# Efficient attention, FNet mix and MLP on one core: second layers of orders 2 to 7 add their results to x by accumulating transfers

## The chip, the core and the metric

The kernel runs on one core of one Trainium2 chip. The metric is the time of one execution on the device in microseconds (us). The kernel before was run 3 times: median 1003.57 us, from 1002.22 to 1005.59. One execution more was taken with the hardware profiler; all views of the trace below are of that one.

## The reference

The inputs are q, k, v of 8 batches, 8 heads, 576 tokens and 64 columns per head, and the weights of an MLP, 512 x 2048 and 2048 x 512; all of it is fp32.

```python
q_s = softmax(q, over the 64 columns); k_s = softmax(k, over the 576 tokens)
kv  = k_s^T v                    # 64 x 64 for each head
x   = q_s kv                     # put side by side: (8, 576, 512)
u   = x + real(fft2(x))          # over tokens and columns
un  = (u - mean(u)) / sqrt(var(u) + 1e-6)
out = u + relu(un @ w_ch1) @ w_ch2
```

The two products of the last line are by far the largest part of the work: 4608 tokens by 512 by 2048, twice.

## The kernel before

**Groups and orders.** The 4608 tokens are taken in nine groups of 512. Group g = 0 to 7 holds 512 of the 576 tokens of batch g; group 8 holds the 64 that each batch leaves over (its tokens lie in tiles called xs, those of a batch in tiles called x). The groups are worked off in the sequence 0 to 6, 8, 7; the place in this sequence is called the *order*, 0 to 8. An order has a first layer (un @ w_ch1, then relu) and a second layer (times w_ch2). In orders 0 and 1 the layers are built in other ways. From order 2 on the second layer is `deep_down` (L1830), a two-level Strassen scheme: seven products on the outer level, m = 1, 6, 5, 7, 2, 4, 3, each of seven smaller products on the inner one. From order 1 on the first layer is a one-level Strassen scheme, `up` (matmuls at L1560), in orders 7 and 8 a deeper one, `wide_up` (matmuls at L1666 and L1716), whose operands are sums formed beforehand (`wide_sums`, L1620). Attention, the FFT and the layer norm of the next batch run beside the layers of an order.

**What is added to x.** The tile x already holds u when the second layer begins. It is addressed as x[u] half d, two halves of tokens u and two halves of columns d, so (u, d) is a quarter of 128 rows by 512 elements: 2 blocks c of 128 rows by 256 elements. An outer product m ends as a tile of the same size, `tile(m)`, that lies in pieces of the large buffer `big`. `into(u, d, m)` (L1866) adds that tile to the quarter (u, d). The calls are listed in `after`, unit by unit: (0,0) from m = 1; (1,0) from m = 4 and (0,0) from m = 2; (0,1) from m = 6; and behind the last unit (1,0) from m = 7, (1,1) from m = 7, (1,1) from m = 5, (0,1) from m = 5, (0,1) from m = 3. These last five have the times +4, +5.5, +7, +8.5 and +10 after the end of the last unit, so they run in the head of the next order, beside its first layer. `sums` (L1870) adds one result tile to another ahead of these. Then `store` (L2103) writes x to the output: the half u = 1 at +9.5, u = 0 at +13, each in two blocks. A block with c = u goes straight out (L2116); one with c other than u goes to a copy in HBM (`mirror`, L2123) and from there, reversed, to the output (L2125). Group 8 has its stores kept back and issued during order 8.

**Who does it.** The variable E in `deep_down` names the engine that adds: GpSimd (POOL) in orders 2 to 6, VectorE (DVE) in orders 7 and 8. In order 7 the last five are handed to POOL nonetheless. Per order there are 9 calls of `into`, so in orders 2 to 7 there are 54: 45 on x by POOL, and on xs 5 by POOL and 4 by DVE.

**What sets the order of the work.** The schedule is written by hand: every step (a Python closure) has a time, all are sorted by it, and the instructions are issued in that sequence under `tc.manual_schedule`. Each engine works off its own part of the sequence in order. Waits between engines, and on transfers, are put in by the framework from the tiles that instructions read and write. So a step that waits holds up everything behind it on its engine's queue, and the times in the list are intentions, not clocks.

**Steps near the change, engine by engine.** *POOL*: besides `into` and `sums` it subtracts maxima from q ahead of the exponential (L818), copies and folds pieces of the transposed layer-norm output unT (L1404, L1410), forms sums of hidden activations (L415, L418), in order 6's end and order 7's head the operands of `wide_up` (tiles F and cd at L1620), and in orders 7 and 8 sums of activations (L1727). The only transfer it issues is one indirect DMA near the end (L2100). *SP* (SyncE) issues nearly all DMA: the loads of both layers' weights into a ring of four buffers in `big` (w1s and the others, L482 to L490: when a buffer has been used, the load for the use four further on is issued), of keys, values and q for the coming batches (L691, L703, L800), and the stores. *TensorE* (PE) runs the matmuls. *DVE* and ScalarE (ACT) take results from PSUM; relu and its sums write to pieces of `big` (L1571, L1572, L1675, L1720), the pieces that earlier held results of the second layer.

Of the kernel before, what the change touches and what calls it, by code (L numbers as in the profile page):

```python
# [43 lines left out]
ALU = mybir.AluOpType  # L44
# [99 lines left out]
class _Block:  # L144
# [1685 lines left out]
    def deep_down(self, g, order):  # L1830

        nc, V, G = self.nc, self.nc.vector, self.nc.gpsimd
        base, last, skip = self.base[order] + NP, order == B, self.first_deep(order)
        E = V if order >= B - 1 else G
# [6 lines left out]
        tile = lambda m: result[m].rearrange("p (c e) n -> p c e n", c=2)  # L1841
# [23 lines left out]

        def into(u, d, m, E=E):  # L1866
            x = self.xs[g, u][:, :, d * HD:(d + 1) * HD].rearrange("p c (e n) -> p c e n", n=P)
            E.tensor_tensor(out=x, in0=x, in1=tile(m), op=ALU.add)  # L1868

        def sums(m, k):  # L1870
            E.tensor_tensor(out=result[m], in0=result[m], in1=result[k], op=ALU.add)
# [91 lines left out]
        def ends(unit, n):  # L1963
# [17 lines left out]
            if n == 3:  # L1981
                plus(out(1), "bc", "u2")

        after = {(1, 2): [(5.2, into, 0, 0, 1), (5.9, into, 0, 0, 2)], (2, 4): [(7, into, 1, 0, 4), (9, into, 0, 0, 2)],
                 (7, 6): [(1, sums, 6, 1), (3, into, 0, 1, 6), (5, sums, 7, 6), *(((7, into, 1, 0, 7), (9, into, 1, 1, 7)) if last else ())],
                 (5, 3): [(4, into, 1, 0, 7, G), (5.5, into, 1, 1, 7, G), (7, into, 1, 1, 5, G), (8.5, into, 0, 1, 5, G), (10, into, 0, 1, 3, G)] if E is V and not last else
                         [(0.6, into, 1, 1, 5), (1.2, into, 0, 1, 5), (1.8, into, 0, 1, 3)] if last else
                         [(4, into, 1, 0, 7), (5.5, into, 1, 1, 7), (7, into, 1, 1, 5), (8.5, into, 0, 1, 5), (10, into, 0, 1, 3)]}
# [307 lines left out]
```

## Time and profile before

| | before |
|---|---|
| median of 3 runs (lowest to highest), us | 1003.57 (1002.22 to 1005.59) |
| the profiled execution, us | 1004.02 |
| its span, us | 1002.1 |
| mean granted clock of TensorE | 1.00 |
| instructions in the span | 20374 |
| moved by DMA | 240.32 MB, 240 GB/s on average |

The span is the time from the first to the last instruction of the profiled execution; the execution's own time has some 2 us around it. Busy times are sums over an engine's instructions and are shares of the span. The time axis of every row starts at the span's start. Across it, the second layers' additions of orders 2 to 6 run from 348.6 to 823.7 us, and those on xs from 870.6 to 910.2.

The part of the page that shows how the work is spread:

```profile
## 2 busy tenths in 40 slices
PE   8999999999999999999999999999999999999998
PEld 6845464888888899889988998899888999999997
DVE  6898899666765887678756886678657866895793
ACT  5585643872468228842775267724782243251310
POOL 4263420357535637664656556564647398352610
PEclk9999999999999999999999999999999999999999
DMA  9987499687989666975769577947656874677473
```

Each digit is the busy share of 25 us in tenths (9 is 90% or more). PE's row is full from the second slice on, at full clock; POOL's row is uneven, with its fullest slice at 800 to 825 us, and the DMA row goes up and down with the layers, highest where the weights of two layers and the inputs of a batch are loaded together.

In rows of the trace the first two columns are the start (us) and the duration (us), then the engine, line, operation, output <- input, shapes and, where it was idle before, the idle time and what ended it in square brackets. "x4" at the end says that four instructions of one form in a row are drawn together. SPq and POOLq are the sequencers that issue transfers.

### The profile page before, as it was taken

Reading aid. Unit: us, or ns where it says so; the run is one execution under the profiler, and the core shown is the slowest. Engines: PE = TensorE matmul, PEld = TensorE weight load, DVE = VectorE, ACT = ScalarE, POOL = GpSimd, SP = SyncE. Lnnn points to the kernel's source line nnn. Section 1 sums busy time; section 2 is a strip of 40 time slices with the busy share of each in tenths; the row PEclk is TensorE's granted clock in tenths of the full one; section 3 lists DMA queues with packets and bytes.
Section 4 is the critical chain, followed back from the end, with each engine's and each line's share of the span. In section 5 each row is a group of like instructions: output and inputs, shape, how many; then the busy total and the mean of one; then the engine's idle time right before and its main releaser. Section 6 shows DMA issues by size and latency. Waiting matters only on the chain.

```text
span 1002.1 us, 20374 instructions
## 1 busy us (share of the span) xinstructions
PE 990.0 (99%) x7754; PEld 856.9 (86%) x7754; DVE 746.5 (74%) x1402; ACT 500.1 (50%) x1290; POOL 506.0 (50%) x498
## 2 busy tenths in 40 slices
PE   8999999999999999999999999999999999999998
PEld 6845464888888899889988998899888999999997
DVE  6898899666765887678756886678657866895793
ACT  5585643872468228842775267724782243251310
POOL 4263420357535637664656556564647398352610
PEclk9999999999999999999999999999999999999999
DMA  9987499687989666975769577947656874677473
GB/s 301 261 282 245 161 253 339 199 245 224 332 295 270 225 233 224 253 256 202 265 196 241 210 263 246 260 175 260 231 174 230 311 251 153 251 268 246 151 268 140
DMA packets 128040, 240.32 MB, mean 240 GB/s; under 512 B 24312, under 2 KB 92152, under 8 KB 117448
## 3 DMA queue, kind: packets, MB, share of 16 engines
q1 hardware_dynamic: 127576, 238.51, 73.0%
q8 instruction: 61, 1.00, 0.4%
q14 instruction: 35, 0.29, 0.1%
q10 hardware_dynamic: 288, 0.26, 0.1%
q0 software_dynamic: 80, 0.26, 0.1%
HBM read 203.87 MB, written 39.06 MB: 242 GB/s over the span
## 4 chain that ended last, share of the span: by engine, by line
PE 87%; DVE 7%; DMA 2%; ACT 2%; issue 1%; SPq 0%; POOL 0%; DVEq 0%; POOLq 0%
PE bb L1560 12%; PE bb L1938 10%; PE ba L1560 8%; PE bc L1560 8%; PE ba L1938 7%; PE bc L1938 7%; PE bb L1888 4%; PE bc L1493 2%; PE bb L2055 2%; PE two L854 2%; PE one L769 2%; PE two L1221 1%; PE two L1278 1%; PE ba L1493 1%; PE ba L1716 1%; PE bc L2055 1%
## 5 line engine op out<-in xcount | busy, mean ns | idle before, releaser
L1560 PE MATMUL bb<-unT,big 128*128 128x256 f32 x576 | 137.8, 381 | 0.0
L1560 PEld LDWEIGHTS bb<-unT,big 128*128 128x128 f32 x576 | 108.4, 190 | 15.6 <-DVE u L1528 0.5
L831 ACT ACTIVATE qT<-q 32x128 f32<-32x128 f32 x384 | 117.9, 307 | 5.9 <-DVE q L821 0.7
L1938 PE MATMUL bb<-big 128*128 128x128 f32 x832 | 101.8, 276 | 0.2 <-DVE u L1945 0.2
L1938 PEld LDWEIGHTS bb<-big 128*128 128x128 f32 x832 | 97.1, 192 | 1.0 <-DVE u L1945 1.0
L1560 PE MATMUL ba<-unT,big 128*128 128x256 f32 x384 | 93.7, 383 | 0.7 <-DMA big<-w1s 0.7
L1560 PE MATMUL bc<-unT,big 128*128 128x256 f32 x384 | 91.2, 380 | 0.1
L1868 POOL TENSOR_TENSOR x<-x,big 128x512 f32<-128x512 f32 x45 | 60.7, 1362 | 45.9 <-DVE big L1945 19.7
L1572 ACT ACTIVATE big<-big 128x512 f32<-128x512 f32 x72 | 44.7, 628 | 78.2 <-DVE big L1571 71.6
L1560 PEld LDWEIGHTS bc<-unT,big 128*128 128x128 f32 x384 | 72.5, 190 | 10.4 <-DVE big L1571 0.5
L1528 DVE TENSOR_TENSOR u<-bb,s 128x512 f32<-128x512 f32 x50 | 34.2, 683 | 63.3 <-PE bb L1560 46.3
L1560 PEld LDWEIGHTS ba<-unT,big 128*128 128x128 f32 x384 | 71.3, 190 | 11.4 <-DMA big<-w1s 0.8
L1938 PE MATMUL ba<-big 128*128 128x128 f32 x648 | 80.1, 276 | 0.0
L1864 DVE TENSOR_TENSOR big<-big 128x512 f32<-128x512 f32 x95 | 78.1, 847 | 0.0
L1938 PEld LDWEIGHTS ba<-big 128*128 128x128 f32 x648 | 75.9, 192 | 0.8
L818 POOL TENSOR_TENSOR q<-q,qm 128x512 f32<-128x512 f32 x24 | 25.8, 1074 | 90.6 <-DVE qm L813 56.9
L1404 POOL COPY unT<-unT 32x256 f32<-32x256 f32 x98 | 43.5, 444 | 46.6 <-DVE unT L1396 42.3
L1404 ACT COPY unT<-unT 32x256 f32<-32x256 f32 x126 | 50.7, 402 | 29.8 <-DVE unT L1396 28.0
L415 POOL TENSOR_TENSOR big<-big 128x512 f32<-128x512 f32 x24 | 30.5, 1270 | 66.6 <-ACT big L1572 66.6
L1938 PE MATMUL bc<-big 128*128 128x128 f32 x400 | 48.9, 275 | 0.0
L1888 PE MATMUL bb<-big 128*128 128x256 f32 x208 | 47.7, 379 | 0.0
L1938 PEld LDWEIGHTS bc<-big 128*128 128x128 f32 x400 | 46.8, 192 | 0.0
(457 smaller groups left out, 2252.4 us busy)
## 6 DMA issues: line engine op xcount, KB each, us to landing
big<-w2d SPq DMA_DIRECT2D x68, 1024.0 KB
big<-w1s SPq DMA_DIRECT2D x64, 896.0 KB
big<-w2s SPq DMA_DIRECT2D x14, 1024.0 KB
big<-in_w_dram SPq DMA_DIRECT2D x21, 512.0 KB
w2d<-big SPq DMA_DIRECT2D x42, 256.0 KB
kb<-in_kT_dram SPq DMA_DIRECT2D x28, 320.0 KB
q<-in_q_dram SPq DMA_DIRECT2D x28, 256.0 KB
vt<-in_v_dram SPq DMA_DIRECT2D x84, 80.0 KB
```

The costliest lines, as they stand in the source:

```text
L415: e1.tensor_tensor(out=to(4), in0=at(2), in1=at(3), op=ALU.add)
L831: nc.scalar.activation(to[t, i * Q:i * Q + Q], one, ACT.Exp)
L1404: copy(to, of)
L1493: nc.tensor.matmul(po[:], lhsT=h[:, f, i * P:(i + 1) * P], rhs=self.w2sb[:, f, :], start=(f == 0), stop=(f == NF - 1))
L1528: plus = lambda t: V.tensor_tensor(out=temp(t), in0=box["bb"][:], in1=box["s1"][:], op=ALU.add)
L1560: nc.tensor.matmul(bank()[:, i, :], lhsT=w[:, WA_AT[m], k * P:(k + 1) * P], rhs=self.unT[g][:, B_AT[m], k, :], start=first and i == 0 and ...
L1572: (0.8, lambda: nc.scalar.activation(hp(i), hp(i), ACT.Relu))]
L1864: (engine or e).tensor_tensor(out=to(o), in0=to(x), in1=to(y), op=op)
L1868: E.tensor_tensor(out=x, in0=x, in1=tile(m), op=ALU.add)
L1888: nc.tensor.matmul(box[name][:, i, :], lhsT=h[p][:, A_AT[m], i * P:(i + 1) * P], rhs=self.stream[n][:, p, :], start=p == 0 and (m != 1 or ...
L1938: nc.tensor.matmul(box[place(unit, n)][:, i, :], lhsT=own(m)(A_AT[n])[:, f, :], rhs=w[:, r // 2, r % 2 * P:r % 2 * P + P], start=first and ...
L2055: nc.tensor.matmul(bank()[:, i, :], lhsT=h[p][:, A_AT[m], i * P:(i + 1) * P], rhs=w[:, p, :], start=first and i == 0 and p == 0, stop=p == ...
```

## The change

In `into`, the engine's addition is replaced by transfers for all second layers but the last: for each of the two blocks c of a quarter, GpSimd issues a DMA from the result tile in `big` to x with addition at the destination. Each moves 128 rows by 256 elements (two runs of 128 elements in the source row), 128 KB. The last order's additions stay on VectorE, which was its E before.

```diff
         def into(u, d, m, E=E):
             x = self.xs[g, u][:, :, d * HD:(d + 1) * HD].rearrange("p c (e n) -> p c e n", n=P)
-            E.tensor_tensor(out=x, in0=x, in1=tile(m), op=ALU.add)
+            if last:
+                V.tensor_tensor(out=x, in0=x, in1=tile(m), op=ALU.add)
+            else:
+                for c in range(2):
+                    G.dma_start(x[:, c], tile(m)[:, c], accum_op=ALU.add)
```

So 54 additions (50 on POOL, 4 on DVE) become 108 accumulating transfers, all issued by POOL, at the same places of the sequence. The sequence of instructions of PE and of SP stays as it was; DVE's loses four instructions in order 7. The waits change: an addition followed its predecessor on the engine's queue, while a transfer that adds to a block waits for the landing of the earlier transfer that adds to the same block; SP's stores of x wait for the landing of the last transfers into it; and whoever writes next to the pieces of `big` that held a result waits until the transfers have read it. Times and the calls of `into` in the list are not touched.

## The prediction

> **What bounds the kernel now.** I read the page's busy times first, then its chain, then who waits for the line that changes.
>
> ```profile
> PE 990.0 (99%) x7754; PEld 856.9 (86%) x7754; DVE 746.5 (74%) x1402; ACT 500.1 (50%) x1290; POOL 506.0 (50%) x498
> PE 87%; DVE 7%; DMA 2%; ACT 2%; issue 1%; SPq 0%; POOL 0%; DVEq 0%; POOLq 0%
> L1868 POOL TENSOR_TENSOR x<-x,big x45: 1259/1272/1725, 348.6 to 823.7; 128x512 f32<-128x512 f32 x45
> L1868 POOL TENSOR_TENSOR xs<-xs,big x5: 1264/1271/1648, 899.7 to 910.2; 128x512 f32<-128x512 f32 x5
> L1868 DVE TENSOR_TENSOR xs<-xs,big x4: 679/683/883, 870.6 to 897.2; 128x512 f32<-128x512 f32 x4
> ```
>
> TensorE (PE) is busy 990.0 of 1002.1 us and 87% of the chain. So there is nothing to win by making another engine lighter: a change can only leave PE's row closed or open holes in it. GpSimd (POOL) is busy half of the time, but that is an average. The question is where its result is wanted at once. The 54 additions that go (45 + 5 on POOL, 4 on DVE) are not in the chain themselves.
>
> **The change part by part.** Each addition becomes two transfers of 128 rows by 256 elements, 108 in all, every one issued on POOL. Two quantities are unknown: I, the time for which one issue holds POOL, and L, the time from the start of an issue until the data has landed. The one transfer that POOL issues in the run before bounds them:
>
> ```profile
> L2100 POOL DMA_INDIRECT out_dram<-x,row x1: 1199/1199/1199, 995.8 to 995.8; - x1
> DMA to landing us min/median/max: 4.6/4.6/4.6
> ```
>
> I take I = 1.2 us and L = 4.6 us. That one also moves 128 rows, but to HBM and without reading its target. Bounds for I: below, the 0.4 us that SP needs for an issue (rows further down); above, 2 x 1.2 = 2.4 us, since a row of the new transfers lies in two pieces of 512 bytes in its source. Bounds for L: below, 2.5 us (a store's bounce copy further down is released within 3.9 us of its issue, in a busy stretch); above, 4.6 + 1.2 = 5.8 us, with the longer issue.
>
> The additions were ordered by their engine's own queue. Transfers are not, so each one waits for the landing of an earlier one that adds to the same quarter of x. In the last five results of a group, m = 7, 7, 5, 5, 3, this bites twice: (1,1) from m = 5 must wait for (1,1) from m = 7, and (0,1) from m = 3 for (0,1) from m = 5. While POOL waits, all that stands behind it in its queue waits too.
>
> *Order 7, POOL's queue.* Here the five additions sit in front of sums that PE takes at once:
>
> ```profile
> 806.70 1.27 POOL L1868 TENSOR_TENSOR x<-x,big 128x512 f32<-128x512 f32 x1
> DVE unT L1410 <- POOL unT L1404: 1.2, 1, 1.2
> 814.67 1.27 POOL L1410 TENSOR_TENSOR unT<-unT 128x512 f32<-128x512 f32 x1 [0.81 <-DVE unT L1410]
> ...
> 818.13 6.87 POOL L1868 TENSOR_TENSOR x<-x,big 128x512 f32<-128x512 f32 x5
> ...
> 826.73 1.28 POOL L1620 TENSOR_TENSOR F<-ft 128x512 f32<-128x512 f32 x1
> 828.09 1.27 POOL L1620 TENSOR_TENSOR cd<-F 128x512 f32<-128x512 f32 x1
> 829.41 1.16 PE L1666 MATMUL bb<-big,cd 128*128 128x128 f32 x8
> ```
>
> The sum into cd ends at 828.09 + 1.27 = 829.36, and the matmuls that read cd start at 829.41: no slack. All from 814.67 to 829.36 is back to back, so every microsecond of POOL is one of PE. New duration of the five: two pairs of issues for m = 7 (the first half of the second pair starts 2I after the beginning); L later its partner for m = 5 may go; the pairs for m = 5 take 4I, of which the last two halves start 2I after that; again L later m = 3 may go, and takes 2I. In all 2I + L + 2I + L + 2I = 6I + 2L = 7.2 + 9.2 = 16.4 us in place of 6.87: +9.5. The single result at 806.70 costs 2I - 1.3 = +1.1 more, which passes on, since the rows show DVE waiting for the copies behind it and POOL for DVE. Together 8I + 2L - 8.2 = **+10.6 us**. It stands alone: DVE's writes into the pieces of big that the transfers still read are released at 833.3 + 1.1 by the same working, before POOL's late cd at 839.9.
>
> [...]
>
> *Orders 3 to 5, SP's queue.* The other heads have room on POOL. What waits there is the store of x, and behind it, on the in-order queue of SP, the weights:
>
> ```profile
> 389.07 1.27 POOL L1410 TENSOR_TENSOR unT<-unT 128x512 f32<-128x512 f32 x1 [1.11 <-DVE km L734]
> 390.30 5.53 POOL L1868 TENSOR_TENSOR x<-x,big 128x512 f32<-128x512 f32 x4
> 400.18 1.04 POOL L818 TENSOR_TENSOR q<-q,qm 128x512 f32<-128x512 f32 x1 [4.34 <-DVE qm L813]
> 401.18 1.27 POOL L1868 TENSOR_TENSOR x<-x,big 128x512 f32<-128x512 f32 x1
> ```
>
> ```profile
> 401.28 0.38 SPq L2123 DMA_DIRECT2D mirror<-x  x1
> 401.70 0.93 SPq L703 DMA_DIRECT2D vt<-in_v_dram  x2
> 402.68 0.95 SPq L2116 DMA_DIRECT2D out_dram<-x  x2
> 403.73 0.40 SPq L490 DMA_DIRECT2D big<-w1s  x1
> 404.18 0.45 SPq L2123 DMA_DIRECT2D mirror<-x  x1
> 404.73 0.42 SPq L800 DMA_DIRECT2D q<-in_q_dram  x1
> 405.20 0.80 SPq L2125 DMA_DIRECT2D out_dram<-mirror  x1
> ```
>
> By the same counting the first half of the last result starts 4I + 2L after 390.30 and lands at 390.30 + 4I + 3L = 390.30 + 4.8 + 13.8 = 408.9. The second store of the pair at 402.68, at about 403.25, waits for it: 5.6 us late, and so are the weights at 403.73, the copy at 404.18 and the load of q. Do they matter? The engines that move the data are full there:
>
> ```profile
> 405.00:417.50 12.50, 12.50 (x93) 10.83 (x92) 7.13 (x17) 11.71 (x34) 8.58 (x9) 1.00 0.90 269
> 417.50:432.50 15.00, 15.00 (x174) 13.10 (x173) 8.91 (x20) 14.43 (x43) 8.05 (x7) 1.00 1.12 235
> SPq L703 <- DMA big<-w1s: 7.0, 2, 3.6
> 432.96 0.31 SPq L703 DMA_DIRECT2D vt<-in_v_dram  x1
> 434.26 0.48 PE L1560 MATMUL ba<-unT,big 128*128 128x256 f32 x1
> ```
>
> (The columns before the end are PE, PEld, DVE, ACT, POOL, the granted clock and the share of the 16 DMA engines.) The load of values at 432.96 waited for the weights to land, and PE uses them at 434.26: a slack of 1.3 us. Put off are 5.6 x 0.90 = 5.0 us of traffic; the unused tenth until 417.5 takes back 1.25; 3.8 - 1.3 = **+2.5 us** of PE.
>
> ```profile
> 495.65 2.96 POOL L1868 TENSOR_TENSOR x<-x,big 128x512 f32<-128x512 f32 x2
> ...
> 509.16 0.90 SPq L2116 DMA_DIRECT2D out_dram<-x  x2
> ...
> 510.00:517.50 7.50, 7.50 (x70) 6.43 (x69) 3.10 (x8) 7.19 (x22) 6.04 (x5) 1.00 0.93 286
> 517.50:520.00 2.50, 2.50 (x13) 2.21 (x12) 1.65 (x3) 0.71 (x3) 0.19 (x1) 1.00 0.43 88
> ...
> 539.92 1.13 PE L1560 MATMUL ba<-unT,big 128*128 128x256 f32 x4 [0.67 <-DMA big<-w1s]
> ```
>
> Order 4 has no slack at all: PE already waits 0.67 us. The last result waits one addition of q (1.4 us) more or less and lands at about 515.2 for a store at 509.7, 5.5 late; 5.5 x 0.93 = 5.1, less 0.5 + 1.4 of unused share, is **+3.2 us**.
>
> ```profile
> 643.83 0.31 SPq L703 DMA_DIRECT2D vt<-in_v_dram  x1
> 646.38 0.92 PE L1560 MATMUL ba<-unT,big 128*128 128x256 f32 x3
> 740.00:747.50 7.50, 7.50 (x36) 6.61 (x35) 4.11 (x8) 7.21 (x24) 4.88 (x5) 1.00 0.07 27
> 921.01 1.27 POOL L1727 TENSOR_TENSOR big<-big 128x512 f32<-128x512 f32 x1 [9.55 <-DVE big L1675]
> ```
>
> Order 5 is built as order 3, with 646.38 - 643.83 = 2.55 us of slack in place of 1.3: 3.8 + 0.2 - 2.55, about **+1.5 us**. In order 6's head the DMA engines fall idle (0.07) before the weights are wanted, so lateness there costs nothing. In order 8's head POOL has 9.55 us of idle time before its next sum; the six results there take about that, and I charge nothing (with the upper bounds, some 5 us). The four results within each second layer cost POOL 1.1 us each in place of gaps of a few us; nothing charged, since the row at 389.07 shows 1.11 us of waiting for DVE just before the next layer. The added traffic itself, 54 x 256 KB = 14 MB beside 240, falls mostly between 390 and 402, where SP issues next to nothing; I charge nothing for it. The 4 additions taken from DVE give back nothing, as PE does not wait there.
>
> **Sum.** 10.6 + 2.5 + 3.2 + 1.5 = 17.8 us on the profiled execution's 1004.0 us (span 1002.1): 1021.8. That execution lies 0.4 us above the median of 1003.57, so 1021.
>
> **The rivals.**
>
> *POOL's queue alone.* If a transfer lands within two issues (L under 2.4 us), POOL never waits: the five cost 10I = 12 us, +5.1, and with the early one +1.1, 6.2 in all. The last result is then issued by 401 and has landed when SP wants it, so no weights are late: 1004.0 + 6.2 - 0.4 = 1010. For it: the target is SBUF. Against: the 4.6 us row.
>
> *Two pieces per row.* With I = 2.4 and L = 5.8 order 7 costs 19.2 + 11.6 - 8.2 = 22.6, and SP's store in order 3 comes at 390.3 + 9.6 + 17.4 = 417.3, 14 us late, 8 more than above in each of three orders: 22.6 + 7.2 + 3 x 8 = 54, 1057 us. Half way lies about 1037. [...]
>
> *Not slower.* If an issue holds POOL as briefly as one holds SP, 0.4 us, two cost less than the addition of 1.27 us. Order 7 is unchanged once 8I + 2L is at most 8.2, so with I = 0.4 at L = 2.5: 1004. Slower begins where 2L exceeds 8.2 - 8I. For it: POOL's share falls from 50%; against: the 1.2 us row.
>
> **How the numbers follow.** The forecast with the sizes it may take (1012 to 1034): 0.50. POOL's queue alone (1007 to 1012): 0.24. Two pieces per row (above 1034): 0.18. Not slower: 0.08. From 1007 to 1040 lie the first two and about a third of the third, 0.80. A measurement of this kernel tells about 0.3%, 3 us, from no change. Faster than that would need PE to gain what it does not lose now: 0.02; within it 0.06; slower 0.92.
>
> **What would show it.** In the profile after: issues of about 1.2 us on POOL; about 10 us between the sum into cd and PE's wait for it in order 7, seen as PE idle before matmuls that read cd; PE waiting for w1s some microseconds at the last part of orders 3 to 5, and SP waiting for the transfers before its stores of x. I am wrong if PE's waits lie in the second layers themselves (then the traffic counts), if order 7 shows none, or if the issues are far from 1.2 us.

## The result and the profile after

The changed kernel takes 1050.84 us (median of 4 runs, 1043.94 to 1052.83) against 1003.56: a ratio of 1.0457, 95% interval 1.0406 to 1.0508. Forecast were 1021 us with a range from 1007 to 1040. So it is slower, as forecast, but by 47 us in place of 17, and outside that range.

The page of the profile after, first its span, busy times and DMA queue, then the chain:

```profile
span 1049.5 us, 20584 instructions
...
PE 1003.5 (96%) x7754; PEld 863.4 (82%) x7754; DVE 730.9 (70%) x1398; ACT 499.5 (48%) x1290; POOL 565.6 (54%) x556
...
q0 software_dynamic: 29456, 14.42, 11.0%
...
PE 62%; DMA 14%; POOL 9%; DVE 9%; issue 3%; ACT 2%; SPq 1%; POOLq 0%; DVEq 0%
```

The execution grew by 47.4 us of span, and the first two lines divide it. PE's idle time rose from 1002.1 - 990.0 = 12.1 to 1049.5 - 1003.5 = 46.0 us: 33.9 us are holes. The same 7754 matmuls also took 1003.5 - 990.0 = 13.5 us longer. The chain, 87% PE before, now has 14% of DMA and 9% of POOL in it. The next view, PE's waits after, names what the holes waited for (us in total, times, longest):

```profile
PE bb L1666 <- POOL cd L1620: 12.4, 1, 12.4
PE bc L1560 <- DVE big L1571: 9.1, 4, 4.7
PE bb L1666 <- DVE big L1675: 3.9, 1, 3.9
PE ba L1560 <- DMA big<-w1s: 2.7, 3, 1.6
```

Only the first was forecast as it came; the fourth, on which 7.2 us of the forecast rested, is small. Most of the 13.5 us of longer matmuls show in windows behind the three longest gaps (columns: window, us, PE, PEld, DVE, ACT and POOL busy, granted clock, DMA share, GB/s):

```profile
421.00:427.00 6.00, 5.97 (x14) 4.82 (x15) 3.96 (x8) 5.77 (x16) 2.27 (x3) 0.51 0.85 274
864.60:870.60 6.00, 5.93 (x28) 5.93 (x28) 1.09 (x2) 0.63 (x1) 5.92 (x8) 0.50 0.36 82
964.00:969.60 5.60, 5.60 (x26) 5.60 (x27) 1.79 (x5) 0.63 (x1) 2.31 (x2) 0.50 0.96 236
```

PE is full in all three and runs at a granted clock of 0.50 or 0.51: each follows a hole, of 4.65, 12.44 and 3.92 us (rows below). Together they hold 17.5 us of matmuls at half the clock; half of that, an estimate of some 9 us, is what the clock costs. The other 4 to 5 of the 13.5 us lie outside these windows and stay unexplained. In the windows behind them (427 to 433, 870.6 to 877 and 969.6 to 975 us) the granted clock is 1.00 again, so the way back took 5.6 to 6 us of busy time here.

Where along the run the time is lost can be read by comparing the start of the same matmul in the two traces. At the matmul that starts at 410 us in the run before, the lag is -0.2; at 745 it is 21.7, at 828 22.8, at 860 38.1, at 1000 45.9. So the heads of orders 3 to 6 with their second layers cost 21.9 us, the head of order 7 15.3, that of order 8 7.8. The steps of this lag lie in the heads.

**Order 7, POOL's queue after** (timeline; the brackets are idle time before and what ended it):

```profile
839.95 4.88 POOL L1872 DMA_DIRECT2D x<-big  x4
846.33 1.20 POOL L1872 DMA_DIRECT2D x<-big  x1 [1.49 <-ACT big L1745]
852.12 3.67 POOL L1872 DMA_DIRECT2D x<-big  x3 [4.59 <-DMA x<-big]
857.14 1.20 POOL L1872 DMA_DIRECT2D x<-big  x1 [1.35 <-DMA x<-big]
859.02 1.20 POOL L1872 DMA_DIRECT2D x<-big  x1 [0.68 <-DMA x<-big]
859.77 0.94 POOL L1657 TENSOR_TENSOR big<-unT 128x128 f32<-128x128 f32 x1
...
863.36 1.26 POOL L1620 TENSOR_TENSOR cd<-F 128x512 f32<-128x512 f32 x1
864.67 1.65 PE L1666 MATMUL bb<-big,cd 128*128 128x128 f32 x6 [12.44 <-POOL cd L1620]
```

Four issues in a row, then POOL stands still for landings, as forecast. The five results hold the queue from 839.95 to 859.77, 19.8 us in place of the forecast 16.4. The next instruction starts 0.75 us after the last issue (859.02 to 859.77): the traced duration of 1.20 is not the time for which POOL is held. The two landings that set this time are those of the fourth issue, the second half of (1,1) from m = 7, and of the eighth, the second half of (0,1) from m = 5. They were issued at 842.16 and 853.58, and the view of each of them alone gives its time to landing:

```profile
DMA to landing us min/median/max: 9.7/9.7/9.7
...
DMA to landing us min/median/max: 4.9/4.9/4.9
```

So one landing of the two was twice as long as the forecast's 4.6 us, and the other was near it.

**Order 3, three queues after.** SP's issues, among them POOL's last transfer; then DVE and PE:

```profile
405.06 5.36 SPq L2120 DMA_DIRECT2D out_dram<-x  x2
409.67 1.20 POOL L1872 DMA_DIRECT2D x<-big  x1 [2.16 <-DMA x<-big]
...
416.45 0.33 SPq L2127 DMA_DIRECT2D mirror<-x  x1
416.88 0.37 SPq L800 DMA_DIRECT2D q<-in_q_dram  x1
...
419.69 0.69 DVE L813 TENSOR_REDUCE qm<-q 128x8 f32<-128x512 f32 x1 [5.66 <-DMA q<-in_q_dram]
420.29 0.68 DVE L1571 TENSOR_TENSOR big<-bc,u 128x512 f32<-128x512 f32 x1
421.03 0.80 PE L1560 MATMUL bc<-unT,big 128*128 128x256 f32 x1 [4.65 <-DVE big L1571]
```

SP's store waits for the landing of the last transfer until 416.45, some 12 us longer than before; q is loaded behind it (416.88, before 404.73), DVE waits 5.66 us for q, and what PE needs (L1571) stands behind that on DVE's queue. The forecast had followed only the weights. The other three holes behind L1571, in orders 4 to 6, come the same way: there too DVE waits 2.6 to 3.4 us for a load of q that SP issued just behind a copy to `mirror`, and does L1571 next.

**Order 8, DVE and PE after:**

```profile
963.20 0.69 DVE L1675 TENSOR_TENSOR big<-bb,u 128x512 f32<-128x512 f32 x1 [4.89 <-DMA xs<-big]
963.95 0.58 PE L1666 MATMUL bb<-big,cd 128*128 128x128 f32 x1 [3.92 <-DVE big L1675]
```

DVE writes into a piece of `big` that a transfer still reads and waits 4.89 us for it.

The transfers themselves, in the view of their line after (duration in ns of those into x, min/median/max; landing times of all):

```profile
L1872 POOL DMA_DIRECT2D x<-big x90: 1181/1678/2721, 348.2 to 859.0; - x90
...
DMA to landing us min/median/max: 3.0/6.6/15.5
```

### The profile page after: what moved, and what is told of

Its sections match the earlier page's. It is cut to its first block, busy times and chain, and to the rows that moved or that the text cites. A ratio compares the mean times of both kernels' runs of the same rounds, so it can differ in the third digit from the quotient of the medians.

```text
span 1049.5 us, 20584 instructions
## 1 busy us (share of the span) xinstructions
PE 1003.5 (96%) x7754; PEld 863.4 (82%) x7754; DVE 730.9 (70%) x1398; ACT 499.5 (48%) x1290; POOL 565.6 (54%) x556
## 3 DMA queue, kind: packets, MB, share of 16 engines
q0 software_dynamic: 29456, 14.42, 11.0%
## 4 chain that ended last, share of the span: by engine, by line
PE 62%; DMA 14%; POOL 9%; DVE 9%; issue 3%; ACT 2%; SPq 1%; POOLq 0%; DVEq 0%
PE bb L1560 7%; DMA x<-big 7%; PE bb L1942 5%; PE bc L1560 5%; PE ba L1560 5%; PE ba L1942 5%; PE bb L1892 4%; DMA big<-w1s 3%; PE bc L1942 3%; POOL x L1872 3%; POOL unT L1404 3%; PE bc L1493 2%; PE bb L2059 2%; DVE big L1864 2%; DMA q<-in_q_dram 2%
## 5 line engine op out<-in xcount | busy, mean ns | idle before, releaser
L1872 POOL DMA_DIRECT2D x<-big x90 | 110.1, 1736 | 80.0 <-DVE big L1949 20.9
L831 ACT ACTIVATE qT<-q 32x128 f32<-32x128 f32 x384 | 117.9, 307 | 18.3 <-DVE q L821 12.2
L1560 PE MATMUL bc<-unT,big 128*128 128x256 f32 x384 | 93.4, 387 | 9.2 <-DVE big L1571 9.1
L1528 DVE TENSOR_TENSOR u<-bb,s 128x512 f32<-128x512 f32 x50 | 34.0, 681 | 56.4 <-PE bb L1560 39.5
L1864 DVE TENSOR_TENSOR big<-big 128x512 f32<-128x512 f32 x95 | 69.5, 758 | 0.0
L818 POOL TENSOR_TENSOR q<-q,qm 128x512 f32<-128x512 f32 x24 | 32.3, 1347 | 68.4 <-DVE qm L813 39.2
L415 POOL TENSOR_TENSOR big<-big 128x512 f32<-128x512 f32 x24 | 33.0, 1375 | 63.9 <-ACT big L1572 63.9
```

Of the source, the lines that this page charges most:

```text
L415: e1.tensor_tensor(out=to(4), in0=at(2), in1=at(3), op=ALU.add)
L818: G.tensor_tensor(out=heads(), in0=heads(), in1=m[:].unsqueeze(2).to_broadcast([P, H, DH]), op=ALU.add)
L831: nc.scalar.activation(to[t, i * Q:i * Q + Q], one, ACT.Exp)
L1528: plus = lambda t: V.tensor_tensor(out=temp(t), in0=box["bb"][:], in1=box["s1"][:], op=ALU.add)
L1560: nc.tensor.matmul(bank()[:, i, :], lhsT=w[:, WA_AT[m], k * P:(k + 1) * P], rhs=self.unT[g][:, B_AT[m], k, :], start=first and i == 0 and ...
L1864: (engine or e).tensor_tensor(out=to(o), in0=to(x), in1=to(y), op=op)
```

## The experiments

**Theory 1:** the loss is made of waits for landings in the heads, passed on by in-order queues, and of PE's lower clock behind each hole. **Theory 2:** it is the added traffic. **Theory 3:** it is POOL's time for issuing. The times stand beside runs of the kernel before on the same chip (medians of 1002.0 to 1003.1 us, 1003.56 for the changed kernel); "lag" is what the profiled execution loses between the same two matmuls, given by their starts in the run before. swap's profiled execution took 1030.5 us, 4 less than its median.

| run | us | ratio to before (95%) | lag 410-745 | 745-828 | 828-860 | 860-1000 |
|---|---|---|---|---|---|---|
| changed kernel | 1050.8 | 1.0457 (1.0406 to 1.0508) | 21.9 | 1.1 | 15.3 | 7.8 |
| heads_add | 1006.8 | 1.0042 (1.0030 to 1.0055) | 1.6 | 1.2 | -0.2 | 0.3 |
| heads3to6_add | 1026.6 | 1.0240 (1.0223 to 1.0257) | 1.1 | 1.9 | 13.8 | 7.0 |
| head7_add | 1029.8 | 1.0261 (1.0244 to 1.0278) | 18.8 | 0.8 | -0.2 | 7.1 |
| head8_add | 1040.0 | 1.0384 (1.0354 to 1.0414) | 19.0 | 0.9 | 14.1 | 0.3 |
| swap | 1034.9 | 1.0329 (1.0311 to 1.0348) | 8.6 | 1.0 | 10.6 | 4.2 |
| sum_early | 1016.7 | 1.0137 (1.0120 to 1.0154) | 3.2 | 0.7 | 4.8 | 3.6 |
| scratch | 1011.5 | 1.0083 (1.0060 to 1.0106) | 0.9 | -0.8 | 3.8 | 1.0 |
| scratch_add | 1019.6 | 1.0187 (1.0154 to 1.0221) | 2.6 | 9.6 | 0.9 | 1.1 |
| copy | 1022.3 | 1.0191 (1.0172 to 1.0209) | 6.9 | -0.6 | 9.6 | 1.5 |
| spread | 1025.5 | 1.0225 (1.0206 to 1.0243) | 7.5 | 9.0 | -0.2 | 6.2 |
| late_stores | 1056.9 | 1.0542 (1.0516 to 1.0568) | 24.8 | 7.6 | 8.3 | 10.8 |
| no_store | 1056.6 | 1040 to 1063, no interval | 20.7 | 1.2 | 17.0 | 6.5 |

### Parts undone

*heads_add*, additions by POOL for the last five results of every order:

```diff
             if last:
                 V.tensor_tensor(out=x, in0=x, in1=tile(m), op=ALU.add)
+            elif m in (7, 5, 3):
+                G.tensor_tensor(out=x, in0=x, in1=tile(m), op=ALU.add)
             else:
```

The other three have the same two lines with a condition more, `num` being the order's number: *head7_add* `num == B - 2 and ...` (order 6's results, in order 7's head), *heads3to6_add* `num < B - 2 and ...`, *head8_add* `num == B - 1 and ...`.

> The last five results of each of orders 2 to 7 (m = 7, 7, 5, 5, 3, in the head of the next order) are added by GpSimd again; the four within the second layer stay transfers (48 of the 108 transfers are left). Theory 1 (the loss is waits for landings in the heads: in POOL's queue, in SP's queue ahead of the stores of x, in writes to big, and PE's lower clock behind each of these gaps): nearly all of it goes, 1004 to 1010 us. Theory 2 (the loss is the added traffic, which slows all loads): the loss goes with the number of transfers, 48/108 of 47 us stays, about 1025. Theory 3 (the loss is POOL's time for issuing): also by number, about 1025, with POOL as the releaser.

> Only order 6's last five results, those in the head of order 7, are added by GpSimd again; 98 of 108 transfers are left. Theory 1: the 12.4 us for which PE waits for the sum into cd and about 3 us at half clock behind it go: 1051 - 15 = about 1036. Theory 2: 10 transfers of 108, 4 us: about 1046.

> The last five results of orders 2 to 5 (in the heads of orders 3 to 6) are added by GpSimd again; those in the heads of orders 7 and 8 stay transfers (68 of 108 are left). By the lags of the traces, 22 us arise in the heads of orders 3 to 6: if each head stands for itself, 1051 - 22 = about 1029. If the heads are linked (a late head making the next one worse, or the traffic of all slowing each), the sum of the three undone parts will not come to the 44 us of all heads together.

> Only order 7's last five results, those in the head of order 8, are added by GpSimd again. Theory 1 (there a write to big waits for the landing of the two transfers that read it, 4 us, PE's clock falls behind that, and w1s come late): 8 us less, about 1043. My charge of nothing: 1051.

heads_add: 1006.8, as theory 1 has it; theories 2 and 3 were 18 us off. Its PE is busy 990.1 us again, so the matmuls' extra time is gone with the holes:

```profile
PE 990.1 (98%) x7754; PEld 857.0 (85%) x7754; DVE 734.1 (73%) x1398; ACT 499.7 (50%) x1290; POOL 532.2 (53%) x526
```

The 48 transfers inside the second layers cost about 4 us. Undone one by one, the heads give back their own lag and leave the others': head7_add 1029.8 (forecast 1036), heads3to6_add 1026.6 (1029), head8_add 1040.0 (1043). The three gains add to 21 + 24 + 11 = 56 us against 44 for all together; all three are taken from the one 1050.8, whose own interval is 5 us to either side, so this doesn't show a link between the heads. Nor do the lags: up to 745 head7_add and head8_add are the changed kernel, and they lose 18.8 and 19.0 us there in place of its 21.9, so some 3 us are the difference between executions.

### The chain of landings

*swap* keeps all transfers and *sum_early* 84 of the 108; both change which waits follow each other:

```diff
# swap (orders 2 to 6)
-  (7, into, 1, 1, 5), (8.5, into, 0, 1, 5), (10, into, 0, 1, 3)
+  (7, into, 0, 1, 5), (8.5, into, 1, 1, 5), (10, into, 0, 1, 3)
# sum_early (orders 2 to 7)
-  (4, into, 1, 0, 7), (5.5, into, 1, 1, 7), (7, into, 1, 1, 5), (8.5, into, 0, 1, 5), (10, into, 0, 1, 3)
+  (4, into, 1, 0, 7), (5.4, sums, 3, 5), (5.5, sums, 5, 7), (8.5, into, 1, 1, 5), (10, into, 0, 1, 3)
```

> In orders 2 to 6 only the sequence of the last five is changed: (0,1)+5 goes ahead of (1,1)+5, so that the transfer with which (1,1)+5 must wait has two more issues of time, and (0,1)+3 waits beside it: one wait of about one landing in place of two, one after the other. Theory 1: in order 7 POOL's chain is about 5 us shorter, in orders 3 to 6 some 1 to 2 us each: 1038 to 1046. Theory 2 or 3 (traffic, issuing): no change, 1048 to 1053.

> In orders 2 to 7 the tiles of m = 3 and 5, and of 5 and 7, are summed by the engine first, so that each quarter gets one transfer behind the last unit and no transfer waits for another one's landing: 6 issues and two additions in place of 10 issues per head, 84 of 108 transfers. Theory 1 (chained landings): 1010 to 1020; what is left is SP's stores behind one landing, and writes to big. Theory 2 (traffic): 84/108 of 47 us, about 1040.

> As the run with sums ahead of the transfers, mended: there the sums came so late in the sequence that the store of x(1) and a write to the result tiles went ahead of them, and the transfers waited for that store. Here the two sums have +5.4 and +5.5. Behind the last unit each quarter gets one transfer, 6 issues and 2 additions per head, no transfer waits for another one's landing; 84 of 108 transfers. Theory 1 (chained landings in POOL's and SP's queues): 1008 to 1018, order 7's head without loss, order 8's with some. Theory 2 (traffic): 84/108 of 47 us, about 1039. If the store of x(0) behind a single landing is enough to hold SP's queue, 1018 to 1030 with the loss in the heads of orders 3 to 6.

swap gives 1034.9, below the 1038 to 1046 of theory 1 and far from the 1048 of the others: traffic, issues and stores are those of the changed kernel, and only two entries of a list changed places. What theory 1 had too small was the gain in the heads of orders 3 to 6: 13 us, where it gave each head 1 to 2; in order 7 it is the 5 us forecast. sum_first was a mistake of mine: its sums had +9.6 and +9.7, behind the store of x(1) at +9.5, so its transfers waited for that store and came too late for what it wrote out. It gave 1042.6 (1.0410, 1.0393 to 1.0428), in POOL's queue of which the idle time "DMA mirror<-x: 12.4, 3" is the new wait; it tells nothing of the chain. sum_early, mended, gives 1016.7: 34 of the 47 us are gone with 84 of 108 transfers still there. POOL's timeline in order 7's head, in this run:

```profile
821.26 2.42 POOL L1872 DMA_DIRECT2D x<-big  x2
822.76 3.99 POOL L1875 TENSOR_TENSOR big<-big 128x512 f32<-128x512 f32 x2
827.04 4.90 POOL L1872 DMA_DIRECT2D x<-big  x4 [0.30 <-POOL big L1875]
830.01 2.43 POOL L1657 TENSOR_TENSOR big<-unT 128x128 f32<-128x128 f32 x1
```

No idle time ends with a landing: 8.8 us from the first issue to the next work (821.26 to 830.01) in place of 19.8. The largest wait left in this run is for the one landing that stayed: DVE's write into `big` in orders 7 and 8, for which PE waits:

```profile
PE bb L1666 <- DVE big L1675: 6.0, 2, 3.2
```

### Traffic, and what accumulating costs

```diff
# scratch: a tile in HBM that nothing reads; scratch_add: the same, with accum_op=ALU.add
-  G.dma_start(x[:, c], tile(m)[:, c], accum_op=ALU.add)
+  to = self.dram.tile([P, 2, P], F32, tag="sink", name="sink", bufs=16)
+  G.dma_start(to[:], tile(m)[:, c])
# copy
-  G.dma_start(x[:, c], tile(m)[:, c], accum_op=ALU.add)
+  G.dma_start(x[:, c], tile(m)[:, c])
```

> The same 108 transfers from the same tiles at the same places of POOL's queue, but as plain copies into 16 rotating tiles in HBM that nothing reads: the results are left out of x. Gone are the waits of a transfer for an earlier one on the same quarter and of SP's stores for landings; issuing, traffic and the waits of writes to big for reads of the transfers stay. Theory 1: order 8's head keeps its 8 us, most else goes: 1010 to 1018. Theory 2 or 3 (traffic, issuing): 1040 or more.

> As the run with copies into tiles in HBM that nothing reads, but accumulating there, so that the DMA engines have the work of additions too; results are left out of x. The earlier run moved its bytes in 5264 packets with 3.7% of 16 engines' time on that queue, in place of 29456 and 11.0%, so it left the traffic open. Theory 1 (waits for landings in x): again 1008 to 1016. Theory 2 (traffic): with 10% or more on that queue, 1030 or more.

> The same 108 transfers to the same quarters of x with the same waits, but as plain copies: the additions are left out, each result overwrites its quarter. If the chain of landings is long because an accumulating transfer takes longer than a copy (6.1 us median to landing, 11.0% of 16 engines' time on its queue), landings shorten to 4 us or less and the time falls to 1025 to 1035. If the landing time is that of the queues in front of it (weights, q), landings stay about 6 us and the time is within 6 us of 1051.

scratch: 1011.5, with 0.9 us lost in the heads of orders 3 to 6, and 1.0 in order 8's, where 8 had been expected to stay; but its copies took a third of the engines' time (3.7% of 16 engines' in place of 11.0%), so scratch_add followed, and its page and its landing times show the load of the changed kernel:

```profile
q0 software_dynamic: 29456, 14.42, 11.7%
```

```profile
DMA to landing us min/median/max: 3.8/7.7/17.6
```

With as many packets and bytes, as many issues and even longer landings, in tiles that nobody adds to or stores from, the heads of orders 3 to 6 lose 2.6 us in place of 21.9. So theories 2 and 3 fall there, with one difference left: these transfers write to HBM, not to SBUF. swap, whose transfers all go to SBUF as in the changed kernel, speaks against the two theories as well. scratch_add still comes to 1019.6, above the 1008 to 1016 of theory 1, by another landing wait, which shows as 9.6 us between 745 and 828: ahead of order 7's cd DVE writes to a piece that a transfer reads, one wait of 8.08 us, for which PE waits 7.9:

```profile
832.62 0.69 DVE L1720 TENSOR_TENSOR big<-bc,u 128x512 f32<-128x512 f32 x1 [8.08 <-DMA sink<-big]
```

copy has all waits of the changed kernel and no additions, and takes 1022.3: 28 of the 47 us hang on the transfers being accumulating ones. Its queue on the page, and its line:

```profile
q0 software_dynamic: 5264, 14.42, 4.0%
```

```profile
L1872 POOL DMA_DIRECT2D x<-big x90: 720/720/925, 348.8 to 837.4; - x90
...
DMA to landing us min/median/max: 2.2/4.7/8.2
```

The same bytes go in (5264 - 80) / 108 = 48 packets per transfer in place of (29456 - 80) / 108 = 272 (80 packets on this queue in the run before, from the indirect transfer), and in 0.040 x 16 x 1021.2 / 108 = 6.1 us of one engine's time in place of 0.110 x 16 x 1049.5 / 108 = 17.1. The landing falls from 6.6 to 4.7 us in the median and from 15.5 to 8.2 at most. I had expected 4 us or less and a time of 1025 to 1035; the landings are longer and the time is shorter. Two waits in a row still cost 9.6 us in order 7.

### Which queue carries it in the heads of orders 3 to 6

```diff
# late_stores
-  store(t + 9.5, 1); store(t + 13, 0)
+  store(t + 17.5, 1); store(t + 21, 0)
# spread: list of orders 2 to 6; and the stores of these orders at + 8
-  (7, into, 1, 1, 5), (8.5, into, 0, 1, 5), (10, into, 0, 1, 3)
+  (7, into, 0, 1, 5), (12, into, 1, 1, 5), (15, into, 0, 1, 3)
# no_store
-  else:
+  elif num > 5:
       store(t + 9.5, 1); store(t + 13, 0)
```

> All transfers stay; the stores of x have times 8 units later (about 7 us), so that on SP the loads of q and of w1s go ahead of the stores that wait for landings. Theory 1 (in orders 3 to 6 it is SP's queue that passes the wait on, to the loads of q and the weights): of the 19 us lost in the heads of orders 3 to 6 some 14 go, about 1037. Rival: the heads of orders 3 to 6 wait for the landings directly, by writes to pieces of big, or for the traffic: within 4 us of 1051.

> In orders 2 to 6 the last five go in the sequence (1,0)+7, (1,1)+7, (0,1)+5, (1,1)+5, (0,1)+3, with the last two at +12 and +15 in place of +8.5 and +10, so that POOL has less to wait for when it gets to them, and the stores of x of these orders are 8 units later (later stores alone gave 1057). Theory 1 with POOL's queue as the carrier in the heads of orders 3 to 6 (sums and subtractions that DVE waits for stand behind the transfers): 12 to 20 us less than the changed kernel, 1031 to 1039. Rival, SP's queue is the carrier there: no better than the 1057 of the later stores, within 6 us.

> The changed kernel without the stores of x in orders 2 to 5 (these rows of the output are left out), so that in the heads of orders 3 to 6 SP waits for no transfer; POOL's queue is as in the changed kernel. If SP's queue carries the loss there (my prediction's step): the lag that these heads add falls from 22 us to 6 or less, about 1033 us. If POOL's queue does (sums and subtractions behind the transfers that wait for landings): 14 us or more of it stay, 1042 or more. In between, both.

late_stores missed: 1056.9 where theory 1, with SP's queue as carrier, wanted 1037. (A few stores of group 8 fall behind the place that issues them and are left out.) spread, with the same later stores but POOL relieved, gave 1025.5, 6 below what I had for it: of the 25 us lag of late_stores up to 745, 17 are gone. Of the 25 us that spread gains on the changed kernel, some 8 lie in order 7: its five results no longer hold up cd, but DVE now waits 6.1 us in L1720 for a transfer that reads its piece, which shows between 745 and 828. no_store has no stores of x at all in orders 2 to 5. Its runs spread from 1040 to 1063, so its time decides nothing; its profile, of an execution of 1050.6 us, shows the path. The heads lose 20.7 us in this one execution, about as much as with stores. Order 4's head, in this run:

```profile
518.97 1.20 POOL L1872 DMA_DIRECT2D x<-big  x1 [4.45 <-DMA x<-big]
525.48 1.20 POOL L1872 DMA_DIRECT2D x<-big  x1 [5.30 <-DMA x<-big]
526.23 1.52 POOL L818 TENSOR_TENSOR q<-q,qm 128x512 f32<-128x512 f32 x1
527.79 0.71 DVE L821 STREAM_TRANSPOSE q<-q 128x512 f32<-128x512 f32 x1 [12.06 <-POOL q L818]
528.42 0.65 DVE L1528 TENSOR_TENSOR u<-bb,s 128x512 f32<-128x512 f32 x1
529.13 1.22 PE L1560 MATMUL bb<-unT,big 128*128 128x256 f32 x2 [8.03 <-DVE u L1528]
```

POOL waits for landings twice, the subtraction from q stands behind, DVE is idle 12.06 us for it with L1528 next in its queue, and PE loses 8.03 us. SP has no part in it. So POOL's queue alone is enough to lose what these heads lose.

In the changed kernel itself both queues lead to q. DVE's waits in the heads of orders 3 to 6 and their second layers (400 to 770 us) tell them apart: the first row is the load of q, which SP issues behind the store, the second the subtraction from q, which stands behind the transfers on POOL:

```profile
DVE qm L813 <- DMA q<-in_q_dram: 20.1, 8, 5.7
DVE q L821 <- POOL q L818: 18.3, 7, 5.0
```

The same two sums in the other runs, from 400 us to behind the matmul that starts at 745 before:

| run | DVE waits for the load of q (SP), us | DVE waits for the subtraction from q (POOL), us | lag 410-745 |
|---|---|---|---|
| before | 1.8 | 3.4 | - |
| changed kernel | 20.1 | 18.3 | 21.9 |
| late_stores | 0 | 30.5 | 24.8 |
| no_store | 0 | 31.2 | 20.7 |
| swap | 9.7 | 3.4 | 8.6 |
| copy | 9.0 | 3.4 | 6.9 |
| spread | 1.1 | 9.9 | 7.5 |

Where SP's wait is taken out, POOL's grows and the loss stays. Where the waits for landings on POOL are fewer or shorter (swap, copy), POOL's wait is that of before, SP's is halved, and about two thirds of the loss go. So neither queue is the carrier alone; the late landings feed both.

## Why the prediction was wrong

- *PE has no slack, a change can only open holes*: right. It left out that the long holes cost twice here. Behind three holes of 3.92, 4.65 and 12.44 us PE ran at a granted clock of 0.50 or 0.51 for some 6 us each, an estimate of 9 of the 47.4 us, for which the sum had no term; in heads_add, where PE's longest wait is 1.3 us, the matmuls take 990.1 us again.
- *The sizes of I and L*: I = 1.2 was too long, 0.72 us by the copies' row, inside the bounds. L = 4.6 with 5.8 as the upper end was too short: 6.6 in the median and up to 15.5. The row that it came from was a single transfer at 995.8, behind the bulk of the loads; no bound allowed for a transfer among them, or for accumulating. No accumulating transfer landed within the 2.4 us that "POOL's queue alone" needed: the quickest took 3.0 us and the median was 6.6, three times the 2.2 us of the quickest plain copy (copy).
- *Order 7, +10.6*: mechanism, place and the wait that ends last were right; the term 6I + 2L was mis-sized. The 19.8 us are two landings of 9.7 and 4.9 us, 0.8 us between landings and issues, and 4.4 us of issuing, where the forecast had 9.2 us of landings and 7.2 of issuing. PE lost 12.4 us for cd and about 3 more to the clock.
- *Orders 3 to 5, +7.2*: this is where the most was missed, and the step that failed is "Do they matter?". The forecast had the store, the weights and the load of q late together, and then asked only for the weights. With landings longer than 4.6 us, the load of q in order 3 came 12.2 us late (416.88 in place of 404.73) in place of 5.6, and DVE waited for it, with PE's next input behind on its queue: 9.1 us of PE's waits in orders 3 to 6, against 2.7 for the weights. "The other heads have room on POOL" failed as well: it holds for gaps of a few us, not for two landings in a row, and the subtractions behind them held DVE for 18.3 us in place of 3.4. Together with order 6, where nothing was charged, these heads cost 21.9 us.
- *Order 8, nothing charged*: wrong by 7.8 us. The cause is not POOL's room, which was asked for, but DVE's write into a piece still being read. The forecast had worked out that wait for order 7, where it was covered (DVE waited 8.5 us and was still ahead of cd), and not for order 8, where PE lost 3.9 us by it, with 1.1 for weights and some 3 for the clock beside.
- *The added traffic, nothing charged*: right for the heads of orders 3 to 6 as far as the DMA engines are merely busier (scratch_add, 2.6 us), wrong in that accumulating transfers land later (6.6 against 4.7 us in the median, 15.5 against 8.2 at most): as plain copies they cost 28 us less (copy).
- *The rivals*: "Two pieces per row" came nearest in time, 1057 in full (half way to it from 1021 is 1039, not the 1037 it names), and by half its reason, so partly by luck: issues were not longer but shorter, landings were longer, in packets of about 480 bytes.

What stays open is why single landings took 9.7 us in order 7 and up to 15.5 us elsewhere: the runs show that copies take less, not what the longest ones waited for.

## What to carry to other kernels

Here the additions were ordered by their engine's queue (the five in order 7 took 6.87 us, back to back); an accumulating transfer into the same place waited for a landing (4.59, 1.35 and 0.68 us in order 7's head, where the five took 19.8), and that wait stood in the issuer's queue ahead of everything behind it. Before replacing one by the other, count the landings that follow each other, list what is queued behind and who waits for that, on every queue to the end, with a landing measured among the other transfers (6.6 us in the median and up to 15.5 here, where the single one of before took 4.6); and add what the clock costs behind holes in PE (0.50 for 5.6 to 6 us behind holes of 3.92 us and more here). Here summing first, so that each place is written once, took back 34 of the 47 us, and leaving the additions on the engine where they stand in the heads took back 44.

## What the runs showed of the hardware

An accumulating transfer of 128 KB between SBUF tiles went in 272 packets and 17.1 us of engine time, a plain one in 48 packets and 6.1. Either held GpSimd for 0.72 to 0.75 us per issue, though the traced duration of the accumulating ones into x was 1.2 to 2.7 us. After holes of 3.92, 4.65 and 12.44 us in TensorE's work the granted clock was about 0.50 for the next 5.6 to 6 us.
